# Identity and masks made by VectorE from a counting row, in place of a loaded table

## The chip, the cores and the metric

The kernel runs on one core of one Trainium2 chip. The metric is device time in microseconds (us) of one execution; the time before is the median of three runs. All views are of one profiled execution of the program. Its engines are TensorE (PE, with its weight loads as PEld), VectorE (DVE), ScalarE (ACT), GpSimd (POOL) and SyncE (SP). A "q" behind a name (ACTq, SPq) means that engine's sequencer, which also issues DMAs.

## The reference

Two stages on inputs q, k, v of 4 batches, 8 heads, 768 tokens and head dimension 64. First a recurrent attention with a decay for each head; then a channel mix of 512 inputs, 1024 hidden units and 512 outputs.

```python
gamma = 1.0 - 2.0 ** (-5.0 - np.arange(H))
for t in range(S):
    state = gamma[None, :, None, None] * state + np.einsum('bhd,bhe->bhde', k[:, :, t], v[:, :, t])
    y[:, :, t] = 1/np.sqrt(D) * np.einsum('bhd,bhde->bhe', q[:, :, t], state)
x = y.transpose(0, 2, 1, 3).reshape(B, S, H * D)
x_prev = shift of x by one token
xk = mu_k * x + (1.0 - mu_k) * x_prev
xr = mu_r * x + (1.0 - mu_r) * x_prev
k = np.maximum(xk @ w_k, 0.0)
out = 1 / (1 + np.exp(-(xr @ w_r))) * (k * k @ w_v)
```

## The kernel before, in words

The 768 tokens of each batch are cut into three blocks of 256, twelve blocks in all. For a block n, q and k are loaded (`lq`, `lk`, lines 229 to 244) and turned by TensorE transposes against an identity matrix (`Tq`, `Tk`, line 279 or 285); ScalarE copies the turned tiles out of PSUM (`Eq`, `Ek`, line 248). v is loaded (`lv`) and scaled by powers of the decay (`vs`, line 260), on VectorE or GpSimd. TensorE makes the scores of tokens within a chunk (`S`, line 346 and others), VectorE multiplies them by a 0/1 mask while it takes them out of PSUM (`M`, lines 354 and 361), and TensorE builds the state from k and scaled v (`C`, line 402 and others), which VectorE adds up (`U`, lines 250 and 426). The sums over masked scores and state (`Y`, `I`, `J`) make the attention's output, which VectorE multiplies by powers of the decay (`D`, line 521). Then the channel mix follows: mixing with the shifted token (`X`, lines 559 and 565), and three matrix products (`K`, `R`, `V`, lines 579 and 589, 619, 631).

Four constant matrices serve the first part, side by side in one fp16 tile `c16` (c_sb in the profile) of 128 partitions by 576 columns: the identity of 128 columns (`ident`, for the transposes), a causal mask of two halves with 128 columns each (`causal`), a mask of 64 columns (`step`) and another causal mask of 128 columns (`below`). A second tile `csm` (csm_sb) holds small fp32 constants, 80 columns: powers of the decay and a small identity. Both are written into the program as tables and loaded at the start (`constants`, lines 669 to 677): ScalarE's queue issues the load of `csm` (line 670), then that of `c16` (line 671), then the two small loads of mu (line 681). SyncE's queue issues the loads of the first half of the first q and k at the same time; they land in a staging tile (k2s, which is not yet needed for its own purpose), from which ScalarE casts them (`cq`, `ck`, line 248). GpSimd's queue issues the load of the first v, then those of the rest of q and k, and all later inputs and weights; these loads may also convert fp32 to fp16.

VectorE's first work is a memset of `zero` (line 672, for the matmuls on zeros, `z`, which keep TensorE busy at the start), some small memsets (lines 674 and 677), and `gy`: the powers of the decay by token. `gy.0` copies four columns out of `csm` (line 713) and doubles the row in seven steps (line 723, each waits for the one before); `gy.1` is the eighth step. Then it scales the first v (line 260).

The order of all work is written out by hand in the string ORDER: each word is an operation with its block and part, `~v`, `~a`, `~p`, `~s` name the engine (VectorE, ScalarE, GpSimd, SyncE), `@` names the PSUM banks. A loop over the words at the end of the kernel issues them one by one. Each engine does its own in this order; between engines, and between dependent instructions of one engine, the framework puts semaphore waits. `constants()` runs ahead of the string.

Of the kernel before, what the change touches and what calls it, by code (L numbers as in the profile page):

```python
# [10 lines left out]
F32 = mybir.dt.float32  # L11
AF = mybir.ActivationFunctionType
ALU = mybir.AluOpType
# [8 lines left out]
WIDE = (2, 3, 4, 5)  # L22
HEADS = ((0, 1), (3, 2), (4, 5), (7, 6))
ORDER = """
gy.0~v mu~a lv.0~p lq.0.0.2~s lk.0.0.2~s ck.0.0.2~a cq.0.0.2~a z.12@6 Tq.0.0.2@0 Tk.0.0.2@1 gy.1~v
z.1@2 mt@2 Ek.0.0.2~a Eq.0.0.2~a S.0.1.0.2@01 S.0.0.0.2@45 me~a lk.0.2.4~p Tk.0.2.4@2 Ek.0.2.4~a
lq.0.2.4~p vs.0~v C.0@67 U.0.0~v Tq.0.2.4@3 Eq.0.2.4~a lq.1~p lk.1~p M.0.1.0.2~v z.2@2 S.0.1.2.4@23
U.0.1~v lv.1~p lk.2~p I.0@01 S.0.0.2.4@67 M.0.0.2.4~v wk.0~p wk.1~p G.0~a z.2@6 Tq.1@6 Eq.1~a vs.1~p
# [55 lines left out]
def kernel(  # L84
# [12 lines left out]
    nc = tc.nc  # L97
    B, H, S, D = q.shape
    dm = H * D
    dff = moe_w_k.shape[1]  # L100
    P = 128
    C = 128
    W = 64
    TM = 2 * C
    NJ = H // 2
    NCO = dm // P
# [4 lines left out]
    LOG = 8  # L111

    gam = 1.0 - 2.0 ** (-5.0 - np.arange(H, dtype=np.float64))
    par = np.arange(P)
    toks = (2 * par[:, None] + np.arange(2)[None, :], par[:, None] + P * np.arange(2)[None, :])
    in_chunk = 2 * (par % W)[:, None] + np.arange(2)[None, :]
    causal_np = (np.arange(C)[None, None, :] >= in_chunk[:, :, None]).astype(np.float16)
    step_np = (np.arange(W)[None, :] >= (par % W)[:, None]).astype(np.float16)
    c16_np = np.concatenate(
        [  # L120
            np.eye(P, dtype=np.float16), causal_np.reshape(P, -1), step_np,
            (np.arange(C)[None, :] >= par[:, None]).astype(np.float16),
        ],
        axis=1,
    )
    gk_np = np.stack(
        [KUP * gam[None, None, :] ** (TM - 1 - t[:, :, None]) for t in toks], axis=1
    )
# [1 line left out]
    gd_np = gam[np.array(HEADS).T[par // D]] ** TM  # L130
    g0_np = 0.125 * KSC / KUP * gam[h_pj] ** (1 - TM)
    pw_np = gam[h_pj][:, None, :] ** (2.0 ** np.arange(LOG)[None, :, None])
    small_np = np.concatenate(
        [x.reshape(P, -1) for x in (gk_np, gd_np, g0_np, pw_np, np.eye(P, 2 * NCO))], axis=1
    ).astype(np.float32)
    c16d = nc.inline_tensor(c16_np, name="c16")
    smalld = nc.inline_tensor(small_np, name="csmall")

    const = ctx.enter_context(tc.tile_pool(name="const", bufs=1))
# [3 lines left out]
    def ring(name, count, shape, dt):  # L143
        tiles = [const.tile([P] + shape, dt, name=f"{name}{i}") for i in range(count)]
        return lambda i: tiles[i % count]
# [16 lines left out]
    OS = ring("os_", 4, [dm], F32)  # L162

    c16 = const.tile([P, 4 * P + W], F16, name="c16_sb")
    csm = const.tile([P, 4 * H + (2 + LOG) * NJ + 2 * NCO], F32, name="csm_sb")
    gy = const.tile([P, NJ, TM], F32, name="gy_sb")
    zero = const.tile([P, P], F32, name="zero")
    mu8 = const.tile([P, P], F32, name="mu8")
    mu = const.tile([P, 2 * NCO], F32, name="mu")
# [5 lines left out]
    ident = c16[:, 0:P]  # L175
    causal = c16[:, P : 3 * P].rearrange("p (i t) -> p i t", i=2)
    step = c16[:, 3 * P : 3 * P + W]
    below = c16[:, 3 * P + W :]
    o = 4 * H
# [1 line left out]
    gd = csm[:, o : o + NJ]  # L181
    g0 = csm[:, o + NJ : o + 2 * NJ]
    pw = csm[:, o + 2 * NJ : o + (2 + LOG) * NJ].rearrange("p (l j) -> p l j", l=LOG)
    ident8 = csm[0 : 2 * NCO, o + (2 + LOG) * NJ :]

    ctx.enter_context(tc.manual_schedule())

# [480 lines left out]

    def constants():
        nc.scalar.dma_start(out=csm, in_=smalld.ap())  # L670
        nc.scalar.dma_start(out=c16, in_=c16d.ap())
        nc.vector.memset(zero, 0.0)
        warm = const.tile([P, 1], F32, name="warm")
        nc.vector.memset(warm, 0.0)
        nc.scalar.activation(out=warm, in_=warm, func=AF.Sigmoid)
        for x in xT:
            nc.vector.memset(x[:, :, 0:1], 0.0)

    def load_mu(e):
        for w, x in enumerate((moe_mu_k, moe_mu_r)):  # L680
            nc.scalar.dma_start(
                out=mu8[w * NCO : (w + 1) * NCO], in_=x.rearrange("(co ci) -> co ci", ci=P)
            )
# [51 lines left out]
    def load_wv(e, h):  # L735
# [7 lines left out]
        "S": scores, "M": masked, "C": state, "U": summed, "G": decayed, "I": inter_off, "Y": intra, "J": inter_on,  # L743
        "D": yout, "dx": differ, "X": mixed, "t": weighed, "K": keys, "Qa": relued, "Qb": squared, "R": gate,
        "s": opened, "V": values, "O": result, "st": store, "gy": powers, "wk": load_wk,
        "wr": load_wr, "wv": load_wv, "mu": load_mu, "mt": trans_mu, "me": copy_mu, "z": zeros,
        "Vc": values_c, "Oc": result_c, "sc": store_c,
    }
    constants()
    for word in ORDER.split():  # L750
        word, _, at = word.partition("@")
# [43 lines left out]
```

## Time and profile before

| what | us |
|---|---|
| median of the runs | 154.84 |
| lowest, highest run | 154.70, 155.07 |
| the profiled execution | 155.0 |
| its span in the profile | 153.2 |
| TensorE busy in it | 143.4 |
| VectorE busy in it | 125.6 |
| ScalarE busy in it | 100.6 |

The page of the profile gives busy time of each engine, the span cut into 40 slices of 3.8 us with a digit for the busy share in tenths, the DMA queues (q0 is GpSimd's, q1 SyncE's, q10 ScalarE's), the chain of work that ended last, and groups of instructions by line. Views of the trace give the same for a window: a timeline row has the start, the length, the engine, the line, the operation, output and inputs, and in brackets the idle time ahead of it with what ended it. A row with x2 or more merges that many instructions in sequence. Rows of DMA issues give the engine that issues, the size, and the us from issue to landing.

### The profile page before, as it was taken

How to read it: one execution, taken by the hardware profiler on the slowest of the kernel's cores; microseconds unless marked ns; L12 is line 12 of the kernel's file. 1: busy time of each engine (PE TensorE's matmuls, PEld its weight loads, DVE VectorE, ACT ScalarE, POOL GpSimd, SP SyncE). 2: the span in 40 equal slices, each digit the busy share in tenths (PEclk: the TensorE clock that was granted, in tenths of full speed). 3: DMA queues.
4: the chain of work that ended last, by engine and by line, in shares of the span. 5: the costliest groups of instructions: out<-in, count | busy, mean ns of one | idle time of the engine just before them, and what ended most of it. 6: DMA issues, size and time to landing. Idle time of an engine off the chain costs nothing.

```text
span 153.2 us, 5520 instructions
## 1 busy us (share of the span) xinstructions
PE 143.4 (94%) x2426; PEld 82.8 (54%) x2426; DVE 125.6 (82%) x201; ACT 100.6 (66%) x187; POOL 55.3 (36%) x65
## 2 busy tenths in 40 slices
PE   7767799999999999999999999999999999999980
PEld 3345477748754554547454655557465445744450
DVE  3466999999999999999999999999789999603150
ACT  3456878899944895879473789879305058996220
POOL 7953998478867109996700000000000000000000
PEclk9999999999999999999999999999999999999997
DMA  4999999999999999999999203220002050100525
GB/s 135 253 223 198 203 230 194 166 247 209 196 166 207 226 257 113 278 283 199 199 200 225 86 0 136 78 75 0 4 4 75 0 205 0 47 22 4 197 90 192
DMA packets 45768, 22.31 MB, mean 146 GB/s; under 512 B 37416, under 2 KB 41392, under 8 KB 45744
## 3 DMA queue, kind: packets, MB, share of 16 engines
q0 software_dynamic: 38704, 14.42, 73.6%
q1 hardware_dynamic: 6592, 7.21, 13.6%
q8 instruction: 19, 0.31, 0.9%
q10 hardware_dynamic: 448, 0.32, 0.7%
q14 instruction: 5, 0.04, 0.1%
HBM read 24.31 MB, written 6.29 MB: 200 GB/s over the span
## 4 chain that ended last, share of the span: by engine, by line
PE 86%; DMA 5%; DVE 3%; ACT 2%; issue 1%; DVEq 0%; POOLq 0%
PE ps L631 27%; PE ps L589 14%; PE ps L619 14%; PE ps L579 14%; DMA v<-in_v_dram 5%; PE ps L285 3%; PE ps L448 2%; PE ps L279 2%; DVE a L361 2%; PE ps L338 1%; PE ps L485 1%; PE ps L325 1%; PE ps L469 1%; PE ps L649 1%; PE ps L373 1%
## 5 line engine op out<-in xcount | busy, mean ns | idle before, releaser
L631 PE MATMUL ps<-wv,k2s 128*128 128x512 f16 x184 | 43.3, 380 | 0.0
L598 ACT ACTIVATE kr<-ps 128x512 f32<-128x512 f32 x48 | 27.4, 596 | 21.4 <-PE ps L589 11.0
L631 PEld LDWEIGHTS <-k2s 128*128 128x128 f16 x184 | 17.0, 98 | 19.3 <-ACT k2s L610 0.2
L637 DVE SCALAR_TENSOR_TENSOR os<-ps,rs 128x512 f32<-128x512 f32 x23 | 15.5, 683 | 12.4 <-ACT rs L625 7.2
L619 PE MATMUL ps<-wr,xr 128*128 128x512 f16 x96 | 23.5, 379 | 0.0
L589 PE MATMUL ps<-xk,wk 128*128 128x256 f16 x192 | 23.4, 273 | 0.0
L579 PE MATMUL ps<-xk,wk 128*128 128x512 f16 x96 | 22.9, 379 | 0.0
L237 POOL DMA_DIRECT2D k<-in_k_dram x20 | 17.9, 909 | 11.2 <-PE ps L391 7.2
L589 PEld LDWEIGHTS <-wk 128*128 128x128 f16 x192 | 18.3, 98 | 4.4 <-issue 0.2
L248 ACT COPY qT<-ps 128x1024 f16<-128x1024 f16 (+1 forms) x13 | 12.4, 950 | 9.6 <-PE ps L285 7.8
L565 DVE SCALAR_TENSOR_TENSOR xr<-dx,mu,xT 128x256 f16<-128x256 f32 (+1 forms) x32 | 18.0, 576 | 0.1
L625 ACT ACTIVATE rs<-ps 128x512 f32<-128x512 f32 x24 | 13.8, 594 | 6.1 <-DVE os L637 3.2
L237 POOL DMA_DIRECT2D v<-in_v_dram x18 | 16.0, 906 | 3.5 <-DVE a L361 1.9
L565 DVE SCALAR_TENSOR_TENSOR xk<-dx,mu,xT 128x256 f16<-128x256 f32 (+1 forms) x32 | 17.1, 580 | 0.2
L361 DVE TENSOR_TENSOR a<-ps,c_sb 128x1024 f16<-128x1024 f32 (+1 forms) x14 | 14.5, 1064 | 0.7 <-PE ps L346 0.4
L610 ACT ACTIVATE k2s<-kr 128x512 f16<-128x512 f32 x24 | 14.6, 626 | 0.2
L579 PEld LDWEIGHTS <-wk 128*128 128x128 f16 x96 | 9.1, 98 | 10.3
L619 PEld LDWEIGHTS <-xr 128*128 128x128 f16 x96 | 9.1, 98 | 10.1 <-DVE xr L565 0.3
L606 ACT ACTIVATE k2s<-kr 128x512 f16<-128x512 f32 x24 | 14.4, 625 | 0.3
L260 DVE TENSOR_TENSOR vs<-v,csm_sb 128x1024 f16<-128x1024 f32 x10 | 12.2, 1216 | 2.7 <-DMA v<-in_v_dram 2.7
L248 ACT COPY kT<-ps 128x1024 f16<-128x1024 f16 (+1 forms) x13 | 12.3, 944 | 2.2 <-PE ps L279 1.6
L536 DVE TENSOR_TENSOR dx<-xT 128x1024 f32<-128x1024 f32 x11 | 13.4, 1222 | 0.3
(71 smaller groups left out, 160.9 us busy)
## 6 DMA issues: line engine op xcount, KB each, us to landing
out_dram<-os SPq DMA_DIRECT2D x23, 256.0 KB, 3.0
v<-in_v_dram POOLq DMA_DIRECT2D x18, 256.0 KB, 7.4
q<-in_q_dram POOLq DMA_DIRECT2D x11, 256.0 KB, 7.9
k<-in_k_dram POOLq DMA_DIRECT2D x21, 128.0 KB, 8.5
v<-in_v_dram POOLq DMA_DIRECT2D x2, 512.0 KB, 7.8
wk<-in_moe_w_k_dram POOLq DMA_DIRECT2D x2, 512.0 KB, 10.4
wv<-in_moe_w_v_dram POOLq DMA_DIRECT2D x2, 512.0 KB, 9.7
wr<-in_moe_w_r_dram POOLq DMA_DIRECT2D x1, 512.0 KB, 8.8
```

Of the source, the lines that this page charges most:

```text
L237: e.dma_start(out=dst[:, :, i * D : i * D + D], in_=src[:, i * P : i * P + P].rearrange("h p d -> p h d"),)
L248: e.copy(out=out, in_=in_)
L361: nc.vector.tensor_tensor(out=a_full(n)[:, i, :, j0:j1], in0=pairs(banks("S", n, i, j0))[:, :, j0:j1], in1=(below if wide(n) else causal[: ...
L565: nc.vector.scalar_tensor_tensor(out=XM[w](k)[:, j, t0:t1], in0=DX(k)[:, j, t0:t1], scalar=mu[:, w * NCO + j : w * NCO + j + 1], in1=x[:, ...
L579: nc.tensor.matmul(banks("K", n, g), lhsT=wk16[:, co, g * P : g * P + P], rhs=XM[0](k)[:, co, :], start=(co == 0), stop=(co == NCO - 1),)
L589: nc.tensor.matmul(pz[:, i, :], lhsT=wk16[:, co, fo * P : fo * P + P], rhs=XM[0](k)[:, co, m * TM + t0 : m * TM + t1], start=(i == 0 and c ...
L598: nc.scalar.activation(out=kr, in_=banks("K", n, g, *u), func=AF.Relu)
L606: nc.scalar.activation(out=k2s[:, n % 3 : n % 3 + 2, g, :], in_=kr, func=AF.Square,)
L610: nc.scalar.activation(out=K2(n)[:, w * g : w * g + w, t0:t1], in_=kr.rearrange("p a t -> p (a t)").rearrange("p (i t) -> p i t", i=w), fu ...
L619: nc.tensor.matmul(banks("R", n, tb), lhsT=XM[1](k)[:, co, t : t + P], rhs=wr16[:, co, :], start=(co == 0), stop=(co == NCO - 1),)
L631: nc.tensor.matmul(banks("V", n, tb), lhsT=K2(n)[:, fo, tb * P : tb * P + P], rhs=wv16[:, fo, :], start=(fo == 0), stop=(fo == NFO - 1),)
L637: nc.vector.scalar_tensor_tensor(out=OS(2 * n + tb), in0=banks("V", n, tb), scalar=1.0 / (KSC * KSC), in1=RS(2 * n + tb), op0=ALU.mult, op ...
```

## The change

`c16` is no longer loaded. `constants` makes a counting row 0 to 127 on VectorE, the same in every partition, in a buffer that is used for results much later (`OS(3)`): one memset and seven additions, each doubling the row. A new operation `masks` (`cm`), first in ORDER and so ahead of `gy.0` on VectorE, makes the five parts of `c16` by comparing the row with a number for each partition; three such columns are appended to `csm`, which grows from 80 to 83 columns. The instructions of TensorE, GpSimd and SyncE stay the same and in the same order; ScalarE issues one DMA less; VectorE has thirteen instructions more.

```diff
--- before.py
+++ after.py
@@ -22,7 +22,7 @@
 WIDE = (2, 3, 4, 5)
 HEADS = ((0, 1), (3, 2), (4, 5), (7, 6))
 ORDER = """
-gy.0~v mu~a lv.0~p lq.0.0.2~s lk.0.0.2~s ck.0.0.2~a cq.0.0.2~a z.12@6 Tq.0.0.2@0 Tk.0.0.2@1 gy.1~v
+cm gy.0~v mu~a lv.0~p lq.0.0.2~s lk.0.0.2~s ck.0.0.2~a cq.0.0.2~a z.12@6 Tq.0.0.2@0 Tk.0.0.2@1 gy.1~v
 z.1@2 mt@2 Ek.0.0.2~a Eq.0.0.2~a S.0.1.0.2@01 S.0.0.0.2@45 me~a lk.0.2.4~p Tk.0.2.4@2 Ek.0.2.4~a
 lq.0.2.4~p vs.0~v C.0@67 U.0.0~v Tq.0.2.4@3 Eq.0.2.4~a lq.1~p lk.1~p M.0.1.0.2~v z.2@2 S.0.1.2.4@23
 U.0.1~v lv.1~p lk.2~p I.0@01 S.0.0.2.4@67 M.0.0.2.4~v wk.0~p wk.1~p G.0~a z.2@6 Tq.1@6 Eq.1~a vs.1~p
@@ -113,16 +113,6 @@
     gam = 1.0 - 2.0 ** (-5.0 - np.arange(H, dtype=np.float64))
     par = np.arange(P)
     toks = (2 * par[:, None] + np.arange(2)[None, :], par[:, None] + P * np.arange(2)[None, :])
-    in_chunk = 2 * (par % W)[:, None] + np.arange(2)[None, :]
-    causal_np = (np.arange(C)[None, None, :] >= in_chunk[:, :, None]).astype(np.float16)
-    step_np = (np.arange(W)[None, :] >= (par % W)[:, None]).astype(np.float16)
-    c16_np = np.concatenate(
-        [
-            np.eye(P, dtype=np.float16), causal_np.reshape(P, -1), step_np,
-            (np.arange(C)[None, :] >= par[:, None]).astype(np.float16),
-        ],
-        axis=1,
-    )
     gk_np = np.stack(
         [KUP * gam[None, None, :] ** (TM - 1 - t[:, :, None]) for t in toks], axis=1
     )
@@ -130,10 +120,10 @@
     gd_np = gam[np.array(HEADS).T[par // D]] ** TM
     g0_np = 0.125 * KSC / KUP * gam[h_pj] ** (1 - TM)
     pw_np = gam[h_pj][:, None, :] ** (2.0 ** np.arange(LOG)[None, :, None])
+    at_np = np.stack([par, 2 * (par % W), par % W], axis=1)
     small_np = np.concatenate(
-        [x.reshape(P, -1) for x in (gk_np, gd_np, g0_np, pw_np, np.eye(P, 2 * NCO))], axis=1
+        [x.reshape(P, -1) for x in (gk_np, gd_np, g0_np, pw_np, np.eye(P, 2 * NCO), at_np)], axis=1
     ).astype(np.float32)
-    c16d = nc.inline_tensor(c16_np, name="c16")
     smalld = nc.inline_tensor(small_np, name="csmall")
 
     const = ctx.enter_context(tc.tile_pool(name="const", bufs=1))
@@ -162,7 +152,7 @@
     OS = ring("os_", 4, [dm], F32)
 
     c16 = const.tile([P, 4 * P + W], F16, name="c16_sb")
-    csm = const.tile([P, 4 * H + (2 + LOG) * NJ + 2 * NCO], F32, name="csm_sb")
+    csm = const.tile([P, 4 * H + (2 + LOG) * NJ + 2 * NCO + 3], F32, name="csm_sb")
     gy = const.tile([P, NJ, TM], F32, name="gy_sb")
     zero = const.tile([P, P], F32, name="zero")
     mu8 = const.tile([P, P], F32, name="mu8")
@@ -181,7 +171,9 @@
     gd = csm[:, o : o + NJ]
     g0 = csm[:, o + NJ : o + 2 * NJ]
     pw = csm[:, o + 2 * NJ : o + (2 + LOG) * NJ].rearrange("p (l j) -> p l j", l=LOG)
-    ident8 = csm[0 : 2 * NCO, o + (2 + LOG) * NJ :]
+    ident8 = csm[0 : 2 * NCO, o + (2 + LOG) * NJ : o + (2 + LOG) * NJ + 2 * NCO]
+    mark = csm[:, o + (2 + LOG) * NJ + 2 * NCO :]
+    count = OS(3)[:, 0:P]
 
     ctx.enter_context(tc.manual_schedule())
 
@@ -668,13 +660,24 @@
 
     def constants():
         nc.scalar.dma_start(out=csm, in_=smalld.ap())
-        nc.scalar.dma_start(out=c16, in_=c16d.ap())
         nc.vector.memset(zero, 0.0)
         warm = const.tile([P, 1], F32, name="warm")
         nc.vector.memset(warm, 0.0)
         nc.scalar.activation(out=warm, in_=warm, func=AF.Sigmoid)
         for x in xT:
             nc.vector.memset(x[:, :, 0:1], 0.0)
+        nc.vector.memset(count[:, 0:1], 0.0)
+        for m in (1 << l for l in range(7)):
+            nc.vector.tensor_scalar_add(out=count[:, m : 2 * m], in0=count[:, 0:m], scalar1=float(m))
+
+    def masks(e):
+        for out, col, op in (
+            (ident, 0, ALU.is_equal), (causal[:, 0], 1, ALU.is_ge), (causal[:, 1], 1, ALU.is_gt),
+            (step, 2, ALU.is_ge), (below, 0, ALU.is_ge),
+        ):
+            nc.vector.tensor_scalar(
+                out=out, in0=count[:, 0 : out.shape[-1]], scalar1=mark[:, col : col + 1], scalar2=None, op0=op
+            )
 
     def load_mu(e):
         for w, x in enumerate((moe_mu_k, moe_mu_r)):
@@ -743,7 +746,7 @@
         "S": scores, "M": masked, "C": state, "U": summed, "G": decayed, "I": inter_off, "Y": intra, "J": inter_on,
         "D": yout, "dx": differ, "X": mixed, "t": weighed, "K": keys, "Qa": relued, "Qb": squared, "R": gate,
         "s": opened, "V": values, "O": result, "st": store, "gy": powers, "wk": load_wk,
-        "wr": load_wr, "wv": load_wv, "mu": load_mu, "mt": trans_mu, "me": copy_mu, "z": zeros,
+        "wr": load_wr, "wv": load_wv, "mu": load_mu, "cm": masks, "mt": trans_mu, "me": copy_mu, "z": zeros,
         "Vc": values_c, "Oc": result_c, "sc": store_c,
     }
     constants()
```

## The prediction

> **What bounds the kernel now.** I read the page from the top: busy time, the 40 slices, then the chain that ended last.
>
> ```profile
> span 153.2 us, 5520 instructions
> PE 143.4 (94%) x2426; PEld 82.8 (54%) x2426; DVE 125.6 (82%) x201; ACT 100.6 (66%) x187; POOL 55.3 (36%) x65
> PE   7767799999999999999999999999999999999980
> PE 86%; DMA 5%; DVE 3%; ACT 2%; issue 1%; DVEq 0%; POOLq 0%
> ```
>
> TensorE is full from about the sixth slice (20 us) to the end; nothing in the change touches what it does there. Only the first 20 us have gaps, and the 5% of DMA in the chain is one transfer. The chain of waits, cut to the first 30 us, shows it:
>
> ```profile
> 1.26 7.03 DMA v<-in_v_dram
> ...
> 8.32 1.24 DVE vs L260
> ...
> 9.60 0.45 PE ps L402 x32
> 10.04 0.36 PE ps L279 x8
> ...
> 10.43 0.59 ACT qT L248
> ...
> 11.07 0.31 PE ps L346 x8
> ...
> 20.50 3.60 PE ps L589 x32
> ```
>
> The columns are start and length in us, and what. The first v lands at 8.29 us, VectorE scales it (line 260) until 9.56, TensorE builds the state from it (line 402), and from there one step hands to the next. At 20.50 the chain enters TensorE (line 589) and stays there. **So the end moves by as much as the end of line 260 at 9.56 moves**, as long as its neighbours move no less. That is the whole question here: does line 260 run earlier or later?
>
> **What the change takes away.** The table is 128 rows of 576 fp16 numbers, 147,456 bytes. Its transfer, by the queues' share in the two stretches 3 to 4 us and 4 to 5 us, and by the issues:
>
> ```profile
> q1 hardware_dynamic: 351, 0.17, 59.1%
> q10 hardware_dynamic: 135, 0.14, 47.4%
> ...
> q0 software_dynamic: 41, 0.17, 53.5%
> q1 hardware_dynamic: 285, 0.14, 47.0%
> q10 hardware_dynamic: 11, 0.00, 1.6%
> ```
>
> ```profile
> 0.74 0.44 SPq L242 DMA_DIRECT2D k2s<-in_q_dram  x1
> 1.23 0.50 SPq L242 DMA_DIRECT2D k2s<-in_k_dram  x1
> 1.17 0.45 ACTq L671 DMA_DIRECT2D c_sb<-c  x1
> ...
> k2s<-in_q_dram SPq DMA_DIRECT2D x1, 256.0 KB, 3.0
> k2s<-in_k_dram SPq DMA_DIRECT2D x1, 256.0 KB, 4.1
> c_sb<-c ACTq DMA_DIRECT2D x1, 144.0 KB, 3.3
> ```
>
> In 3 to 4 us ScalarE's queue (q10) moves 0.14 MB, the table, and takes 47.4% of sixteen engines for one microsecond: 0.47 us of all engines. GpSimd's queue (q0), which carries v, moves nothing in that stretch; its first packets come in 4 to 5 us, although the issue of v ended at 2.29 us. So v stands behind the table and behind the two k2s loads, and without the table it should start, and land, about 0.5 us earlier. Bounds: the engine that finishes last gives the table more (q lands at 0.74 + 3.0 = 3.7, the table at 1.17 + 3.3 = 4.5, k at 1.23 + 4.1 = 5.3: 0.8 us each), so 0.8 above; and nothing below, if v's landing is set by something else on that last engine. I take 0.5, the share of all engines: v lands at 7.8. The new table of small constants grows by 12 bytes a partition, 1.5 KB in 40 KB: nothing.
>
> The neighbours move with it. The casts of the first k and q wait for the k2s landing at 5.3, which was behind the table too. One DMA issue less on ScalarE (0.45 us) moves its table load and the loads of mu forward; ScalarE then waits for k2s anyway (2.18 us idle ahead of its first cast), so this is worth nothing by itself.
>
> ```profile
> 5.33 0.62 ACT L248 CAST k<-k2s 128x512 f16<-128x512 f32 x1 [2.18 <-DMA k2s<-in_k_dram]
> 6.52 0.41 PE L279 MATMUL ps<-c_sb,q 128*64 128x128 f16 x8 [0.90 <-ACT q L248]
> 8.32 1.23 DVE L260 TENSOR_TENSOR vs<-v,csm_sb 128x1024 f16<-128x1024 f32 x1 [2.67 <-DMA v<-in_v_dram]
> 10.43 0.68 DVE L361 TENSOR_TENSOR a<-ps,c_sb 128x512 f16<-128x512 f32 x1
> ```
>
> The transposes (line 279) no longer wait for the table but for VectorE's identity; they are due at 6.5 now, 6.0 afterwards. The masks are first read at 10.43.
>
> **What the change adds.** On VectorE, ahead of the powers (lines 713 and 723) and of line 260: a memset of one column, seven additions that double the counting row (each waits for the one before), then, once the small constants have landed, five comparisons. Queued behind them in order: the powers, line 260, then everything that VectorE does for the first block. All are one-source instructions, SBUF to SBUF. These are the rows to price them by; the last two are one tile's instructions with shortest, median and longest duration in ns:
>
> ```profile
> 0.84 0.17 DVE L672 MEMSET zero<- 128x128 f32 x1 [0.84 <-PEq L779]
> 0.96 0.09 DVE L677 MEMSET xT<- 128x4 f32 x3
> 2.62 0.43 DVE L713 COPY gy_sb<-csm_sb 128x4 f32<-128x4 f32 x1 [1.57 <-DMA csm_sb<-csmall]
> 3.08 2.57 DVE L723 TENSOR_TENSOR gy_sb<-gy_sb,csm_sb 128x4 f32<-128x4 f32 x8
> ...
> L723 DVE TENSOR_TENSOR gy_sb<-gy_sb,csm_sb x8: 167/208/692, 3.1 to 5.0; 128x4 f32<-128x4 f32 x1, 128x8 f32<-128x8 f32 x1, 128x16 f32<-128x16 f32 x1, 128x32 f32<-128x32 f32 x1
> L713 DVE COPY gy_sb<-csm_sb x1: 431/431/431, 2.6 to 2.6; 128x4 f32<-128x4 f32 x1
> ```
>
> _Undisturbed price._ A small dependent step costs about 0.2 us (the shortest of line 723 is 167 ns, and steps follow each other at some 0.03 us). Seven make 1.4 us, from 1.06 to 2.5, before the constants land at 2.6: free. Five comparisons over 128 columns, at the memset's 0.17 us, make 0.85 us. The powers would end at 5.65 + 0.85 = 6.5, still 1.3 us ahead of a v at 7.8. In this case the change costs nothing, and the gain of 0.5 us arrives.
>
> _Disturbed price._ The copy in line 713 moves four numbers per partition and takes 431 ns; the two-source steps behind it, of the same size, take 167. Put beside GpSimd's own instructions, which write the descriptors of the loads:
>
> ```profile
> 1.26 1.03 POOL L242 DMA_DIRECT2D v<-in_v_dram  x1 [0.82 <-POOLq L779]
> 2.29 0.76 POOL L242 DMA_DIRECT2D k<-in_k_dram  x1
> 3.04 1.64 POOL L242 DMA_DIRECT2D q<-in_q_dram  x2
> 4.65 0.90 POOL L242 DMA_DIRECT2D k<-in_k_dram  x1
> 5.51 0.93 POOL L242 DMA_DIRECT2D v<-in_v_dram  x1
> 6.39 1.79 POOL L237 DMA_DIRECT2D k<-in_k_dram  x2
> 8.58 0.76 POOL L730 DMA_DIRECT2D wk<-in_moe_w_k_dram  x1 [0.39 <-DMA v<-in_v_dram]
> ```
>
> The copy starts at 2.62, in the middle of GpSimd's k issue, and ends at 3.05, where that issue ends (2.29 + 0.76 = 3.05). The two-source steps of line 723 run through the next three issues with no such delay. I read it so: a one-source SBUF-to-SBUF instruction of VectorE that meets a GpSimd issue waits until close to that issue's end. It is one instruction, so this is an inference. The Trainium skill's page "SBUF — State Buffer", section "Who interferes with whom", has such a rule: copies, casts and tensor_scalar in a two-port mode share a pair of ports with GpSimd under an exclusive lock, and the second to come waits in full. The copy's 431 ns beside the issue that ends with it agrees. By that rule the additions and comparisons would be held too.
>
> Two or three additions are done before v's issue takes hold (1.06, 1.26, 1.46 are their starts; I count two). Eleven one-source instructions then stand against GpSimd: five additions, five comparisons, the copy. GpSimd's issues follow each other without a gap and end at 2.29, 3.05, about 3.8, 4.65, 5.5, 6.4, about 7.3 and 8.2. How many get in at one boundary decides. One at least does: the copy did. More than that depends on how long an issue runs before it holds VectorE up; the copy came 0.33 us after its issue's start and was held, so at most about 0.33 us at the head and a little at the tail are free, one or two steps of 0.2 us. _At two per boundary_ the eleventh passes at the sixth, 6.4 us, and the powers' 2.57 us end at 9.1 (6.44 + 0.03 + 2.57 = 9.04, and a little for the copy). Line 260 starts at 9.1 in place of 8.32: **0.8 us late**. The stall on v that covered all this (2.67 us idle) is then gone, and the powers are what line 260 waits for.
>
> In the other direction GpSimd's issues may be held by VectorE for up to 0.2 us at a boundary. That costs nothing directly: v's descriptors stand ready from 2.29 and are first moved after 4 us, and the later loads queue behind each other until 20 us.
>
> The sum, two per boundary: 155.0 us for the profiled execution (span 153.2, and 1.8 us around it) plus 0.8 is 155.8. The median of the runs before is 154.84, 0.16 below the profiled one; against it the forecast is 154.84 + 0.8 = **155.6 us**.
>
> **The rivals.**
>
> _The table's time comes through (faster)._ The hold is short, or passes three or more instructions at a boundary: 3, 3, 3 and 2 end at the fourth boundary, 4.65, the powers at 7.4, and v's landing at 7.8 rules again. Time 154.84 - 0.5 = 154.3, with 0.8 at most 154.0. For it: the comparisons do not wait for each other, and three memsets that do not either take 0.09 us together, so a short run of comparisons could pass one boundary. Against it: the copy's 0.26 us over its neighbour. The point from which it decides: the powers must end before 8.3, so the eleventh must pass before 5.6, the fifth boundary.
>
> _One per boundary (much slower)._ Eight of the eleven pass by 8.2; then GpSimd waits for v (0.39 us idle ahead of its wk issue), the last three follow at 0.2 us each, to 8.8, and the powers end at 11.4. Line 260 is 3.1 us late: 157.9. The additions wait for each other, which speaks for it; that only a few need to go in pairs to undo it speaks against it.
>
> _The edit does not do what it is for._ v's landing is held by the last DMA engine or by GpSimd's own start and stays at 8.3, and VectorE is done by then; or the powers end near 8.3 by chance (five boundaries: 5.5 + 2.7 = 8.2). Time 154.8.
>
> **How the numbers follow.** Two per boundary and its surroundings (powers ending from 8.6 to 9.9, 155.1 to 156.5): 0.38. One per boundary, or nearly: 0.14. The table's time comes through: 0.34. No change: 0.14. A measurement of this kernel can tell about 0.2%, 0.3 us, from no change. Slower by more than that is 0.38 + 0.14 = 0.52, faster 0.34, within it 0.14. The cases stand on both sides, so the range is wide: the likeliest one's own is 155.1 to 156.5; the whole is 154.2 to 157.3, which leaves out the part of the gain beyond 0.6 us and the full price of one per boundary, some 0.15 together.
>
> **What would show it.** In the changed kernel's profile: no q10 traffic between 3 and 4 us and the first k2s cast near 4.8 (the table's time); v's landing near 7.8; the additions and comparisons of some 0.1 to 0.2 us each, ending near 3.4 (undisturbed), or with several of 0.4 to 0.9 us that end with GpSimd's issues (held); the wait ahead of line 260 still on the DMA, or gone, with the powers directly ahead of it. The forecast is wrong if the comparisons are done by 4.7, or if line 260 starts before 8.3. It is also wrong if line 260 moves and the end does not follow, which would mean a slack between 10 and 20 us that the chain does not show.

## The result, and the profile after

| what | before | after |
|---|---|---|
| median of 21 runs each, us | 155.07 | 154.47 |
| ratio, 95% interval | | 0.9961 (0.9947 to 0.9975) |
| span of the profiled execution, us | 153.2 | 152.6 |
| first scaling of v starts | 8.32 | 7.53 |
| state step on TensorE starts | 9.60 | 8.94 |

The changed kernel is faster by 0.39%, 0.6 us. The forecast was 155.6, slower; the time lies inside the range, which was wide enough to hold both answers, on the side of the rival in which the table's time comes through. Ratios leave out runs more than 1.5% above the fastest of the same kernel (seven of twelve where the masks are loaded late, six of ten in the kernel before with fewer zeros), so for such kernels the ratio and the median don't agree.

The line numbers of after differ: 248 is 240 now, 260 is 252, 279 is 271, 346 is 338, 361 is 353, 402 is 394, 565 is 557, 589 is 581, 698 is 701, 713 is 716, 723 is 726. New are 671 (the additions) and 678 (the comparisons). The page of the changed kernel begins:

```profile
span 152.6 us, 5532 instructions
PE 144.1 (94%) x2426; PEld 82.9 (54%) x2426; DVE 128.7 (84%) x214; ACT 100.6 (66%) x187; POOL 55.3 (36%) x65
```

VectorE has 3.1 us more to do (125.6 before), and the span is 0.6 shorter: the added work is real, and it is covered. Where it lies, the timeline of VectorE over the first 14 us shows (start, length, group, idle time ahead of it):

```profile
1.10 1.97 DVE L671 TENSOR_SCALAR os<-os 128x1 f32<-128x1 f32 x7
3.11 1.62 DVE L678 TENSOR_SCALAR c_sb<-os,csm_sb 128x128 f16<-128x128 f32 x5
4.19 0.56 DVE L716 COPY gy_sb<-csm_sb 128x4 f32<-128x4 f32 x1
4.78 2.57 DVE L726 TENSOR_TENSOR gy_sb<-gy_sb,csm_sb 128x4 f32<-128x4 f32 x8
7.53 1.23 DVE L252 TENSOR_TENSOR vs<-v,csm_sb 128x1024 f16<-128x1024 f32 x1 [0.18 <-DMA v<-in_v_dram]
```

The last row decides. Line 252 still waits for v and not for the powers, but the idle time ahead of it went from 2.67 us to 0.18. The powers end at 7.35; v is there at 7.5. The cover is nearly used up, and it just held. In another profile with the same start (GpSimd's scaling later, below) it did not quite: line 252 starts at 7.36 right behind the powers, with no wait for v.

The other half of the sum, the transfers, stands in the queues' share in the stretches 3 to 4 us and 4 to 5 us, and in the first cast on ScalarE:

```profile
q1 hardware_dynamic: 641, 0.32, 105.5%
q0 software_dynamic: 4, 0.02, 14.3%
q10 hardware_dynamic: 10, 0.00, 1.1%
...
q0 software_dynamic: 39, 0.16, 80.5%
```

```profile
4.68 0.62 ACT L240 CAST k<-k2s 128x512 f16<-128x512 f32 x1 [2.01 <-DMA k2s<-in_k_dram]
```

ScalarE's queue (q10) moves next to nothing between 3 and 4 us; SyncE's queue (q1) moves 0.32 MB there in place of 0.17. GpSimd's queue, with v, moves its first 0.02 MB there, and has 80.5% of the engines between 4 and 5 us in place of 53.5%, although it moves no more bytes in that stretch (0.16 MB against 0.17). The first cast starts at 4.68, 0.65 earlier, and v lands 0.79 earlier.

That 0.79 did not reach the end whole. The state step on TensorE's timeline is

```profile
8.94 0.45 PE L394 MATMUL ps<-vs,k 64*64 64x64 f16 x32
```

and the chain of waits, cut to the first 30 us, begins on TensorE now, not with v (it sets its steps at the ends of the work that they follow, so the state step stands at 9.01 there):

```profile
1.06 5.46 PE ps L701 x6
6.52 0.59 PE ps L271 x16
...
8.25 0.42 PE ps L338 x16
8.67 0.34 PE ps L271 x8
9.01 0.38 PE ps L394 x32
...
19.86 3.60 PE ps L581 x32
```

In this profile the matmuls on zeros, which keep TensorE busy at the start, end at 6.52. In the kernel before they ended at 5.62 (1.06 + 4.56, the first row here) and TensorE then waited 0.90 us for the cast:

```profile
1.06 4.56 PE L698 MATMUL ps<-zero 128*128 128x512 f32 x6 [1.06 <-DVE xT L677]
```

Now the cast is early and the zeros are what the transposes stand behind; copies, scores, transposes and state follow one after the other without a gap. v scaled is ready at 8.76, the state step starts at 8.94. It has moved by 0.66, the entry into line 581 (589 before) by 0.64, from 20.50 to 19.86, and the span by 0.6.

### The profile page after: what moved, and what is told of

It is laid out like the page before. It is cut to its first block, busy times and chain, and to the rows that moved or that the text cites. A ratio compares the mean times of both kernels' runs of the same rounds, so it can differ in the third digit from the quotient of the medians.

```text
span 152.6 us, 5532 instructions
## 1 busy us (share of the span) xinstructions
PE 144.1 (94%) x2426; PEld 82.9 (54%) x2426; DVE 128.7 (84%) x214; ACT 100.6 (66%) x187; POOL 55.3 (36%) x65
## 4 chain that ended last, share of the span: by engine, by line
PE 91%; DVE 3%; ACT 2%; issue 1%; DVEq 0%
PE ps L623 27%; PE ps L581 14%; PE ps L611 14%; PE ps L571 14%; PE ps L701 4%; PE ps L277 3%; PE ps L440 2%; PE ps L271 2%; DVE a L353 2%; PE ps L330 1%; PE ps L477 1%; ACT qT L240 1%; PE ps L317 1%; PE ps L461 1%; PE ps L641 1%; PE ps L365 1%
```

## The experiments

The kernel before was run again beside each group: its medians were 155.28 (first four), 155.22 (next four) and 154.94 (last four).

**The table's bytes, put back.** The changed kernel with the table loaded as well, at its old place, into a buffer that is not used until much later:

```diff
         nc.scalar.dma_start(out=csm, in_=smalld.ap())
+        nc.scalar.dma_start(out=RS(3).bitcast(F16)[:, 0 : 4 * P + W], in_=c16d.ap())
         nc.vector.memset(zero, 0.0)
```

> The changed kernel with the 147 KB table loaded as well, by ScalarE's queue at its old place, into a buffer that nothing reads before it is written again; VectorE's masks stay. Theory A (the gain is the table's bytes ahead of the first k and v): v lands near 8.3 us again, the first cast starts near 5.3, line 260's scaling starts near 8.3, and the time is that of the kernel before, 155.1 us, with ratio 0.998 to 1.002; VectorE's new work then costs nothing, because it ends near 7.4. Rival B (the gain comes from elsewhere: TensorE waiting on VectorE in place of a transfer, or the order of the start): the gain stays, 154.5 us. Rival C (the held comparisons do cost, and the table's removal pays more than 0.6): slower than before, 155.4 us or more.

Measured: 154.96, ratio to before 0.9978 (0.9958 to 0.9997). Its timelines of VectorE and TensorE (line 252 is 263 in this kernel, 394 is 405) have:

```profile
8.21 1.23 DVE L263 TENSOR_TENSOR vs<-v,csm_sb 128x1024 f16<-128x1024 f32 x1 [0.76 <-DMA v<-in_v_dram]
9.49 0.45 PE L405 MATMUL ps<-vs,k 64*64 64x64 f16 x32
```

With the bytes back, v's scaling is back at 8.21 (8.32 before, 7.53 after) and the state step at 9.49. VectorE made its masks all the same, and waited 0.76 us for v. So the early landing comes from the bytes, and not from anything that the edit does on VectorE. The time is less clear: by the ratios a gain of 0.22% is left of the 0.39%, and the two intervals overlap. What holds this remainder isn't shown.

**Only the masks' bytes, moved out of the way.** The kernel before, with the 32 KB identity at its old place and the 115 KB of masks behind the casts on ScalarE's queue:

```diff
-        nc.scalar.dma_start(out=c16, in_=c16d.ap())
+        nc.scalar.dma_start(out=ident, in_=c16d.ap()[:, 0:P])
...
+    def load_masks(e):
+        nc.scalar.dma_start(out=c16[:, P:], in_=c16d.ap()[:, P:])
```

> The kernel before, with the table loaded in two parts: the identity (32 KB) at the old place, the masks (115 KB) by ScalarE's queue behind its first two casts. No work is added to VectorE. Theory A: most of the bytes are out of the way of k and v, so v lands near 7.6, and TensorE's first transposes follow the matmuls on zeros; the time is that of the changed kernel, 154.5 us, within 0.2. Rival C (the held comparisons take a part of the gain): 154.2 us or less, since VectorE has nothing ahead of line 260. Rival D (late masks delay the loads behind v, or their landing ends last ahead of line 361): 154.8 us or more.

Measured: median 157.63, ratio 1.0037 (0.9994 to 1.008). Two rows of its VectorE:

```profile
7.61 1.23 DVE L260 TENSOR_TENSOR vs<-v,csm_sb 128x1024 f16<-128x1024 f32 x1 [1.94 <-DMA v<-in_v_dram]
...
10.21 0.69 DVE L361 TENSOR_TENSOR a<-ps,c_sb 128x512 f16<-128x512 f32 x1 [0.41 <-DMA c_sb<-c]
```

The start of v's scaling moves by 0.71 us without any work added to VectorE: the bytes again. As a way to the same gain it failed: the masks came last of all and VectorE waited 0.41 us for them. The interval of the ratio reaches from no change to 0.8% slower, and the median is 2.35 us above that of before. The profiled execution (158.71 us) has both of the things that the next experiment meets: the granted clock is 0.50 from 12.66 to 16.08 us, after 3.41 us with TensorE busy for 2.19, and line 565's four steps take 3.58 us in place of 1.67. What each is worth here isn't shown.

**The comparisons twice.** The changed kernel with the word `cm` twice at the head of ORDER, ten comparisons in place of five:

```diff
-cm gy.0~v mu~a lv.0~p
+cm cm gy.0~v mu~a lv.0~p
```

> The changed kernel with the five comparisons made twice. Theory A with the hold as the trace shows it (comparisons of 0.24 to 0.74 us that wait for GpSimd's issues): five more take 1.0 to 1.7 us, the powers end at 8.4 to 9.0 in place of 7.35, line 260 starts there in place of 7.53, and the end moves by that less the 0.2 us of slack ahead of line 402: 155.1 to 155.8 us. Rival E (line 260 is not what decides any more, there is slack behind it): no change against the changed kernel, 154.5 us. Rival F (comparisons are not held as a rule, 0.17 us each, 0.85 in all): powers at 8.2, 154.9 us.

Measured: 158.07, ratio 1.0158 (1.0119 to 1.0198).

```profile
3.10 2.71 DVE L678 TENSOR_SCALAR c_sb<-os,csm_sb 128x128 f16<-128x128 f32 x10
...
8.42 1.22 DVE L252 TENSOR_TENSOR vs<-v,csm_sb 128x1024 f16<-128x1024 f32 x1
...
9.69 0.45 PE L394 MATMUL ps<-vs,k 64*64 64x64 f16 x32 [1.19 <-DVE vs L252]
```

Line 252 now starts straight behind the powers at 8.42, with no wait on v: the cover is gone, and line 252 starts 0.89 us later than in the changed kernel. That is the mechanism of the forecast, reached with five more instructions to be held. The state step is 0.75 us later than in the changed kernel. But by the two ratios the time is some 3 us longer (0.0197 of 155), much more than the step. Two things happen behind it. TensorE idles 1.19 us, and over the stretches 8.75 to 12.16 and 12.16 to 15.57 us the windows show (length, busy time of PE, PEld, DVE, ACT and POOL, then the granted clock):

```profile
8.75:12.16 3.41, 2.05 (x62) 1.33 (x62) 2.48 (x5) 1.56 (x5) 0.92 (x2) 1.00 1.61 250
12.16:15.57 3.41, 2.90 (x40) 1.90 (x43) 1.65 (x3) 1.33 (x3) 2.10 (x2) 0.50 1.72 191
```

After a stretch in which TensorE was busy for 2.05 of 3.41 us, the clock granted in the next is 0.50. The second thing is a meeting at 35 us, VectorE's four steps of line 557 with GpSimd's scaling of block 3's v. The changed kernel first, then the comparisons twice:

```profile
33.85 1.67 DVE L557 SCALAR_TENSOR_TENSOR xk<-dx,mu,xT 128x256 f16<-128x256 f32 x4
...
35.89 1.91 POOL L252 TENSOR_TENSOR vs<-v,csm_sb 128x1024 f16<-128x1024 f32 x1
```

```profile
35.68 3.20 DVE L557 SCALAR_TENSOR_TENSOR xk<-dx,mu,xT 128x256 f16<-128x256 f32 x4
...
35.14 2.27 POOL L252 TENSOR_TENSOR vs<-v,csm_sb 128x1024 f16<-128x1024 f32 x1
```

In the changed kernel VectorE is done (35.52) before GpSimd begins. In this one they meet, and the four steps take 3.20 us in place of 1.67.

**The clock held up.** To part the two, the same kernel with three more matmuls on zeros ahead of the state step, in TensorE's idle time:

```diff
-lq.0.2.4~p vs.0~v C.0@67
+lq.0.2.4~p vs.0~v z.3@6 C.0@67
```

> The run with the comparisons made twice, and three small matmuls on zeros (about 0.9 us) put in the 1.19 us in which TensorE waited there for line 260. Theory K (of that run's loss only 0.7 us is the late line 260; the rest is TensorE's clock, which drops to half for 3.4 us at 12.2 us after a stretch with TensorE busy for 60%): the clock stays up and the time is that of the changed kernel plus 0.7, 155.0 to 155.4 us. Rival L (the late line 260 itself costs it all, by the order of what follows): 157.5 to 158.5 us again.

Measured: 157.27, ratio 1.0145 (1.0115 to 1.0176). The clock stays at 1.00 (over 7.10 to 10.51 and 10.51 to 13.92 us, TensorE is busy for 2.5 of 3.41 us in each), but only 0.8 us of the time comes back between the medians, 0.2 us between the ratios, and the intervals overlap. The expectation that the clock was all the rest, 155.0 to 155.4 us, failed. What the clock alone is worth isn't settled, also because the state step starts at 10.30 here, 0.61 later than with the comparisons twice. The meeting is still there:

```profile
35.13 3.28 DVE L557 SCALAR_TENSOR_TENSOR xk<-dx,mu,xT 128x256 f16<-128x256 f32 x4
...
35.00 1.91 POOL L252 TENSOR_TENSOR vs<-v,csm_sb 128x1024 f16<-128x1024 f32 x1
```

**The meeting taken away.** GpSimd's scaling of block 3's v left out of three kernels: the last one, before, and after. Their state is then built from an older block's scaled v, so they don't do all the work and serve for timing alone.

```diff
-K.2.3@4 M.4.1~v M.4.0~v Qa.2.3~a Qb.2.3~a lk.6~p S.3.1@67 M.3.1~v S.3.0@01 vs.3~p C.3@23 U.3.0~a
+K.2.3@4 M.4.1~v M.4.0~v Qa.2.3~a Qb.2.3~a lk.6~p S.3.1@67 M.3.1~v S.3.0@01 C.3@23 U.3.0~a
```

> The run with the comparisons made twice and the gap filled, without GpSimd's scaling of block 3's v (its state is built from an older block's scaled v, so the output of the blocks behind it differs). In the run with it, VectorE's four steps of line 565 at 35.1 us meet GpSimd's scaling at 35.0 to 36.9 and take 3.28 us in place of 1.67. Theory M (two-source instructions of VectorE and GpSimd that both read SBUF hold each other up; the start's delay of 1.0 to 1.3 us costs more than itself only because it brings them together): line 565's four take 1.67 us, and the time is 155.2 to 155.8 us. Rival (the order of what follows costs it, not this meeting): 157 us again.

> The kernel before without GpSimd's scaling of block 3's v (its state is built from an older block's scaled v, and GpSimd's later loads start 1.9 us sooner). Theory M: the runs above 156 us vanish, since the meeting that made them is gone, and the rest stay at 155.0 to 155.2 us. Rival: the tail stays, 1 to 3 runs in 12 above 156 us.

> The changed kernel without GpSimd's scaling of block 3's v, as in the run on the kernel before. Theory A with M: the change is worth the same 0.5 to 0.6 us as with the scaling, 154.4 to 154.6 us and no runs above 156 us. Rival N (part of the 0.6 us is that the changed kernel meets the scaling less often, even in runs not counted as disturbed): the difference between this run and the one on the kernel before falls to 0.3 us or less.

| without the scaling | median, us | ratio to before | state step starts | span |
|---|---|---|---|---|
| masks twice, filled | 155.39 | 1.0031 (1.0014 to 1.0047) | 10.31 | 153.5 |
| before | 155.00 | 1.0 (0.9978 to 1.0021) | 9.69 | 153.5 |
| after | 153.86 | 0.9929 (0.9906 to 0.9952) | 8.78 | 151.9 |

In the first of them line 557 is back at 1.67 us (its VectorE's row), and the time is 1.9 us shorter than with the scaling. TensorE's waits show the way to the end: with the scaling it waits 0.9 us for what line 557 writes, and between 28 and 46 us never for GpSimd's scaling, and it is busy for 8.93 of the 10 us from 30 to 40; without it there is no such wait, and it is busy for all 10. Not all of the 1.9 us is the meeting, since the changed kernel, whose profile has none, gains 0.4 to 0.6 us by the same edit. Against the changed kernel, the doubled and filled one loses 3.0 us with the scaling (157.27 against 154.28) and 1.5 us without it (155.39 against 153.86). So the late step and the meeting are worth some 1.5 us each there; what the clock adds in the comparisons twice stays open.

```profile
35.12 1.67 DVE L557 SCALAR_TENSOR_TENSOR xk<-dx,mu,xT 128x256 f16<-128x256 f32 x4
```

Before loses nothing and gains nothing by leaving the scaling out; after without it is faster than before without it by 1.1 us. That refutes the thought that the change wins only because it moves the 557 steps clear of GpSimd. In these two profiles the state step lies 0.91 us apart, not 0.66, which is most of that gap; why the rest is there stays open, since leaving out the scaling also lets GpSimd's later loads start 1.9 us sooner.

The first and the third make the cleanest test of the prediction's main step, since nothing meets in either and neither shows a dropped clock behind the first matmuls. From their chains:

```profile
10.31 0.45 PE ps L394 x32
...
21.22 3.60 PE ps L581 x32
```

```profile
8.78 0.45 PE ps L394 x32
...
19.69 3.60 PE ps L581 x32
```

The state step is 1.53 us apart, the entry into line 581 1.53, the spans 1.6, the medians 1.53. With the clock held and the meeting gone, the end does move by as much as the step.

**Fewer matmuls on zeros.** Since the zeros had become the head of the chain in the changed kernel's profile, the changed kernel with two of the six large ones (in the profile's count) left out, and the same in the kernel before:

```diff
-cm gy.0~v mu~a lv.0~p lq.0.0.2~s lk.0.0.2~s ck.0.0.2~a cq.0.0.2~a z.12@6 Tq.0.0.2@0
+cm gy.0~v mu~a lv.0~p lq.0.0.2~s lk.0.0.2~s ck.0.0.2~a cq.0.0.2~a z.8@6 Tq.0.0.2@0
```

> The changed kernel with two matmuls on zeros at the start in place of three (z.8 for z.12). In its trace those three run until 6.52 us, in the kernel before until 5.62, and the first transposes follow at once. Theory A (these matmuls, slowed by a clock that comes up later, take a part of the gain): transposes start near 5.8, when the casts are done, line 402 then waits for line 260 alone, and the end comes 0.2 us earlier, 154.2 to 154.3 us. Rival G (with less work at the start the clock comes up later still, and the first small matmuls run at half speed): no gain or slower, 154.5 to 155.0 us.

> The kernel before with two matmuls on zeros at the start in place of three. In its trace TensorE stands idle for 0.90 us between them and the first transposes, so they end nothing last. Theory G, from the run with fewer zeros on the changed kernel (its first matmuls took 0.64 us per eight where they take 0.41 otherwise, until 16 us): the start has no stretch of 3.4 us in which TensorE is busy throughout, the clock comes up only near 16 us, and the time is 157.5 to 158.5 us. Rival (that loss belonged to the changed kernel): 155.1 us as before.

Measured: 157.95 for after, ratio 1.0168 (1.0119 to 1.0217), and 158.92 for before, ratio 1.0116 (1.0073 to 1.0158). TensorE's timeline of the first of them:

```profile
6.35 0.64 PE L271 MATMUL ps<-c_sb,q 128*64 128x128 f16 x8 [1.51 <-ACT q L240]
```

The zeros end at 4.84 and the transposes start when the cast is there, but eight of them take 0.64 us in place of 0.41: TensorE still runs at its slower pace, and the state step starts at 9.72. In the kernel before with four zeros the granted clock drops instead, over 8.89 to 12.30 us, after 3.42 us with 1.57 busy:

```profile
5.47:8.89 3.42, 1.57 (x36) 1.10 (x38) 1.54 (x3) 2.25 (x6) 3.10 (x5) 1.00 1.45 181
8.89:12.30 3.41, 3.38 (x70) 2.10 (x70) 1.93 (x4) 1.89 (x5) 1.11 (x2) 0.50 1.54 246
```

So the zeros that now stand in the way can't simply be cut: with two fewer, the clock came up later in the one profile and dropped again in the other. The loss is not the clock's alone, though. The four mixing steps of VectorE meet GpSimd's scaling in both (it begins at 35.98 and 36.03):

```profile
36.56 3.19 DVE L557 SCALAR_TENSOR_TENSOR xk<-dx,mu,xT 128x256 f16<-128x256 f32 x4
...
35.10 3.53 DVE L565 SCALAR_TENSOR_TENSOR xk<-dx,mu,xT 128x256 f16<-128x256 f32 x4
```

TensorE waits 0.8 and 1.4 us for what these steps write. As with the comparisons twice, a later start seems to bring the two together; how the loss divides between clock and meeting isn't shown.

**The hold by itself.** The changed kernel with the comparisons in a two-source form, the column as a broadcast second tensor:

```diff
-            nc.vector.tensor_scalar(
-                out=out, in0=count[:, 0 : out.shape[-1]], scalar1=mark[:, col : col + 1], scalar2=None, op0=op
+            nc.vector.tensor_tensor(
+                out=out, in0=count[:, 0 : out.shape[-1]],
+                in1=mark[:, col : col + 1].to_broadcast([P, out.shape[-1]]), op=op,
```

> The changed kernel with the five comparisons in a two-source form (the counting row against the number's column, repeated along the row). Theory H (one-source instructions from SBUF to SBUF are held to the end of a GpSimd issue, two-source ones are not): the additions and the copy keep their long ones, no comparison takes over 0.35 us, the five take 1.1 to 1.5 us, and the time is that of the changed kernel, since v's landing still ends later. Rival (anything on VectorE is held): comparisons of 0.4 to 0.75 us as before.

Measured: 154.40, ratio 0.9948 (0.992 to 0.9976). The comparisons of the changed kernel and of this one, by shortest, median and longest duration in ns:

```profile
L678 DVE TENSOR_SCALAR c_sb<-os,csm_sb x5: 236/402/743, 3.1 to 4.0; 128x128 f16<-128x128 f32 x4, 128x64 f16<-128x64 f32 x1
```

```profile
L678 DVE TENSOR_TENSOR c_sb<-os,csm_sb x5: 219/284/291, 3.4 to 4.1; 128x128 f16<-128x128 f32 x4, 128x64 f16<-128x64 f32 x1
```

The two-source form is not held, 291 ns at most, and the five take 1.03 us in place of 1.62. Part of that is the start: the small constants landed later here, and the one-source form begun as late as this (3.39, in after without the scaling) took 1.37. The time is that of the changed kernel: what the hold costs lies under the wait for v.

**The changed kernel again,** as it is, beside these:

> The changed kernel itself, beside the others on one chip. Theory A and the spread of its earlier runs: 154.3 to 154.6 us, ratio 0.995 to 0.998; v lands between 7.4 and 8.0 and line 260 starts at its landing or at the powers' end, 7.4, whichever is later.

Measured: 154.28, ratio 0.995 (0.9926 to 0.9973). The gain repeats.

**GpSimd's scaling later.** An attempt at a better kernel: the changed one with GpSimd's scaling of block 3's v behind its next load, and the state step that reads it moved back too:

```diff
-S.3.1@67 M.3.1~v S.3.0@01 vs.3~p C.3@23 U.3.0~a
-Qb.2.2~a K.2.1@4 Qa.2.1~a
+S.3.1@67 M.3.1~v S.3.0@01 lq.6~p vs.3~p
+Qb.2.2~a K.2.1@4 C.3@23 U.3.0~a Qa.2.1~a
```

> The changed kernel with GpSimd's scaling of block 3's v issued one load later (about 0.9 us), and on TensorE the state that waits for it behind one product of the mixing (K.2.1), so that line 565's steps end before it also in late runs. Theory M: the undisturbed time stays, 154.3 to 154.6 us, and the runs above 156 us go. Rival O (the later scaling itself ends last for the state): 154.8 us or more.

Measured: 154.89, ratio 0.999 (0.9971 to 1.0009). Line 557 is clear of GpSimd (33.78 to 35.46 against 36.64), but TensorE's waits of 30 to 45 us, where the changed kernel has none, read

```profile
PE ps L581 <- ACT tg L240: 0.4, 1, 0.4
PE ps L581 <- ACT kr L590: 0.2, 1, 0.2
```

which is 0.6 us, the whole gain. No kernel of these runs beats the changed one by more than its interval, of those that do all the work.

## Why the prediction was wrong

The prediction named its own sign of being wrong, a line 260 that starts before 8.3; it started at 7.53.

- _The end moves with line 260, if its neighbours move no less._ Held for the gain, with the neighbours as the limit: 0.79 at line 260, 0.66 at the state step, 0.6 at the end. Held at 1.53 to 1.53 where clock and meeting were taken out. For a loss it is only a lower bound: 0.75 us at the step became some 3 us.
- _The table's time, 0.5 us, between 0 and 0.8._ The mechanism was right, as the landing in the kernel with the table kept shows. The size was at the upper bound in the two profiles compared here: 0.79 for v and 0.65 for the casts.
- _One-source instructions are held by GpSimd's issues._ Right, though read from a single row. The fourth addition took 566 ns in place of 174, the longest comparison 743, the copy 559; the two-source form was not held.
- _Two pass per boundary._ **This is the step that failed.** Two additions were to be done ahead of v's issue, and the eleven instructions left to need six boundaries, to 6.4. The rows of VectorE's additions (the first three; the fourth and fifth; the seventh), of its last comparison and of the copy, and GpSimd's issues beside them:

```profile
1.10 0.56 DVE L671 TENSOR_SCALAR os<-os 128x1 f32<-128x1 f32 x3
1.70 0.77 DVE L671 TENSOR_SCALAR os<-os 128x8 f32<-128x8 f32 x2
2.72 0.35 DVE L671 TENSOR_SCALAR os<-os 128x64 f32<-128x64 f32 x1
3.99 0.74 DVE L678 TENSOR_SCALAR c_sb<-os,csm_sb 128x128 f16<-128x128 f32 x1
4.19 0.56 DVE L716 COPY gy_sb<-csm_sb 128x4 f32<-128x4 f32 x1
...
1.26 1.03 POOL L234 DMA_DIRECT2D v<-in_v_dram  x1 [0.82 <-POOLq L782]
2.29 0.77 POOL L234 DMA_DIRECT2D k<-in_k_dram  x1
3.04 1.64 POOL L234 DMA_DIRECT2D q<-in_q_dram  x2
4.64 0.91 POOL L234 DMA_DIRECT2D k<-in_k_dram  x1
```

  Three additions are done by 1.66, although v's issue began at 1.26, so ten instructions are left, not eleven. The fourth addition is held to the end of that issue (2.27, 2.29); the fifth and sixth follow it inside the next issue's first 0.4 us. The seventh is held to 3.07, where that next issue ends (2.29 + 0.77 = 3.06), and the first comparison, which begins at 3.11, goes right behind it. Three more comparisons pass near 3.8, inside the merged row of two issues. The last comparison is held to 4.73, and the copy, begun 0.2 us behind it, ends at 4.75 with it: both pass the boundary at 4.65. Three, two, three and two, and that is all; the powers end at 7.35. The rival had 3, 3, 3 and 2, the fourth boundary, and the powers at 7.4. With the ten at two per boundary, by the prediction's own sum, the fifth boundary (5.5) and 2.6 us of powers would still have come to 8.1, behind v's 7.5. Eleven at the measured rate would have needed the fifth too. So the count and the rate were one boundary too many each, and only both together bring the sixth (6.4) down to the fourth (4.65). The rival's 7.4 came out, at 7.35, but by eleven at three per boundary where it was ten at 3, 2, 3 and 2; that closeness is luck. For the rate I had the row of three memsets that did not wait for each other in 0.09 us, and gave more weight to the copy. One held instruction tells that there is a hold, and not how many pass when it ends.
- _What is late next: the powers._ Wrong too, in a smaller way. The powers left 0.18 us of the 2.67. What was late next, in the profile of the changed kernel, were TensorE's matmuls on zeros, which the prediction did not mention: in the kernel before they ended 0.90 us ahead of need, and the casts came 0.65 forward. It is a near tie: in after without the scaling, where the zeros end at 6.16, the chain begins with v again (6.21 us from 1.27).
- _The constants' 1.5 KB and the issue less on ScalarE are worth nothing._ No run tests them alone.
- _GpSimd's issues may be lengthened._ They were not: 1.03, 0.77, 1.64 and 0.91 us against 1.03, 0.76, 1.64 and 0.90.

## What to carry to other kernels

When work is put in the shadow of a wait, two numbers decide: how long the shadow still is after the change, since the change shortens the wait too, and what the added work costs at that very place beside its neighbours; a rate that a single row does not show is bounded from both ends, and the choice between them is a guess. Ask which engine is next when a load comes early: here matmuls that were there only to keep a clock up. And a delay near the start can cost several times its length when it lets a clock drop or moves two engines onto each other later on, so a loss can't be read from the first chain alone.

## What the runs showed of the hardware

- **The length of the gap between GpSimd's issues, for VectorE.** One-source SBUF-to-SBUF instructions take 0.15 to 0.29 us and are held to 0.74; two or three pass at each end of an issue, dependent ones too, in some 0.4 us; GpSimd is not lengthened (1.03, 0.77, 1.64, 0.91 us against 1.03, 0.76, 1.64, 0.90). The Trainium skill's page that the prediction names, "SBUF — State Buffer", agrees on the hold; of the length of the gap, and of GpSimd going on unhindered, this case's rows alone tell. The two-source form, 0.22 to 0.29 us, passes freely.
- **VectorE with two SBUF sources beside GpSimd reading SBUF.** The four steps of line 557 (565 in before) take 1.67 us alone and 3.19 to 3.58 beside GpSimd's 1.9 us scaling in the profiles shown here. The scaling's own time is 1.91 when it began just before them (35.00 against 35.13) or after them, and 2.27 when it had begun 0.54 us before. The Trainium skill's page "SBUF — State Buffer", section "Who interferes with whom", says that a VectorE instruction with two SBUF inputs contends with a GpSimd instruction that reads SBUF; the rows agree. The same section gives, as inferred, that the two-source form leaves the port that descriptor writing needs alone; the powers and the two-source comparisons agree.
- **TensorE's clock at the start.** Six equal matmuls on zeros take 4.56 us in the one profile, 5.46 and 4.38 in others with the same instructions on TensorE there (after, and after with the table kept). It is not the change that lengthens them: the kernel before shows 5.49 in its run without GpSimd's scaling. In their durations the change of pace is seen (shortest, median, longest in ns, before and then after):

```profile
L698 PE MATMUL ps<-zero x6: 592/1021/1221, 1.1 to 5.0; 128*128 128x512 f32 x6
```

```profile
L701 PE MATMUL ps<-zero x6: 1031/1061/1222, 1.1 to 5.5; 128*128 128x512 f32 x6
```

  Before, the last ones already run at the quick pace; after, all six are slow. The Trainium skill's page "TensorE: Matmul & The Clock Gate", Part 1, says that the clock comes up after some 3.4 us of activity, in a window that does not start with the kernel, so that it differs from run to run. These lengths for the same instructions agree. So part of the 0.13 us between v's gain and the state step's may be this one execution's phase, and only the medians speak for the kernel. With four zeros in place of six the changed kernel takes 1.7% longer than before, though 0.8 us of that is TensorE's wait at the meeting near 36 us. The profile's row of clock digits (PEclk) shows nines in the first two slices of all these kernels, also of that one, whose transposes still run at the slow pace; so a slow start is read from durations.
